# Sinkhorn attention and feed-forward on one core: the first half of w_in loaded in 16 equal pieces ahead of four pieces of queries

## The chip, the cores and the metric

The kernel runs on one core of a Trainium2 chip. The metric is the device time of one execution in microseconds (us). Five engines work side by side: TensorE (PE, with its weight loads shown as PEld), VectorE (DVE), ScalarE (ACT), GpSimd (POOL) and SyncE (SP). POOL and SP also issue DMA transfers, which 16 DMA engines carry out.

## What is computed

For each of 4 batches and 8 heads (768 tokens, head size 64) an 8x8 matrix is normalised five times over rows and columns. It mixes the 8 blocks (96 tokens each) of keys and values, and each block of queries attends to its mixed block. The result, 3072 tokens by 512, then goes through a feed-forward layer.

```
P = sort_net;  5 times: P = exp(P - max);  P /= rows' sums;  P /= columns' sums
k_s, v_s = P mixes the 8 blocks of k and of v
attn = softmax(q_b @ k_s.T / 8) @ v_s            per block of 96 tokens
h = x @ w_in;  g = s * relu(h)**2 + b;  out = g @ w_out
```

w_in is 512 x 2048 and w_out is 2048 x 512, both in fp32. The inputs' DMAs, issued by POOL, convert to bf16 on the way, so a piece that is 128 KB in memory lands as 64 KB. The profile counts what lands.

## The kernel before, in words

The order of every engine's work is written out by hand. A batch is cut into two halves of 384 tokens; a half is one "tile" t of the feed-forward layer, so there are eight tiles.

**Start.** PE runs dummy matmuls (`warm`, L131) while DVE and ACT normalise the 8x8 matrices (L257 to L272). In the meantime POOL issues loads in this order: the first half of the first queries (`load_qh(0, 0)`, L148 and L103), the first keys in 3 pieces (L149, L92), some small constants, and then the loads that the change touches (L163 to L171, all issued by `load_wi`, L141, and `load_qh`, L103). After them come memsets for the next batch (L172 to L175), the scalars s and b (L177), w_out in 4 pieces (L180), and values, keys and queries of batch 1 (L181 to L184).

**The queue.** Every transfer that POOL issues takes one of eight semaphores in turn. So a transfer can be issued only when the eighth one before it has landed; POOL waits there, and everything behind it on POOL's queue waits too.

**First half of batch 0.** L501 to L529: the mixing matrix (`build_pd`, L278), transposed queries (`q_banks`, L233), mixed keys (L303, L315) and values (L325), scores (L357, L375), the exponentials on ACT (L361, L380), weighted values (`p_piece`, L399), their transposes (`t_piece`, L416), and the first parts of the feed-forward product with w_in (`part`, L450), which use columns 0 to 511 of w_in. Dummy matmuls (L393, L445) are mixed in.

**Feed-forward, tile 0.** `ffn1(0)` (L593) walks over eight steps i, each with 256 columns of w_in. Step 0 is followed by `q_banks(0, 1)`, which reads the second half of the first queries. Steps 2 and 3 need columns 512 to 1023, steps 4 to 7 the second half of w_in. The second half of batch 0's attention is laid between the steps. `ffn1(1)` follows, with `make_bias` (L554) in step 4, which needs all of w_out; then `ffn2(0)` and `ffn2(1)` (L474) with batch 1's keys, values and queries between them, and so on for the other batches.

The array `wi` holds w_in as `[128, 4, 2048]`: index 1 is the quarter a of the 512 rows. `load_wi(f0, f1, a)` loads columns f0 to f1 of one or more quarters. W8 is 256 columns and W4 is 512.

Of the kernel before, what the change touches and what calls it, by code (L numbers as in the profile page):

```python
# [22 lines left out]
def kernel(  # L23
# [18 lines left out]
    NHP = H // 2  # L42
# [54 lines left out]
    def load_qh(b, half, parts=1):  # L97
        if b not in QH:
            QH[b] = rawp.tile([128, H, CQ, D], BF, tag="rawq", name="qh")
        qv = q[b].rearrange("h (f p c) d -> f p h (c d)", f=2, c=CQ)  # L100
        for h in range(0, H, H // parts):
            hs = slice(h, h + H // parts)
            nc.gpsimd.dma_start(  # L103
                out=QH[b][half * 64:(half + 1) * 64, hs].rearrange("p h c d -> p h (c d)"),
                in_=qv[half][:, hs])
# [33 lines left out]
    def load_wi(f0, f1, al=None):  # L139
        al = slice(0, NHP) if al is None else al  # L140
        nc.gpsimd.dma_start(out=wi[:, al, f0:f1], in_=wiv[:, al, f0:f1])  # L141
# [18 lines left out]
    ones = const.tile([128, 32], BF)  # L160
    W4 = d_ff // 4
    W8 = d_ff // 8
    for a in range(NHP):  # L163
        load_wi(0, W8, slice(a, a + 1))
    for a in range(0, NHP, 2):
        load_wi(W8, W4, slice(a, a + 2))
    for c in range(1, 4):
        for a in range(NHP):
            load_wi(c * W4, (c + 1) * W4, slice(a, a + 1))
        if c == 1:  # L170
            load_qh(0, 1, 2)  # L171
    nc.gpsimd.memset(ones, 1.0)  # L172
    nc.gpsimd.memset(VP[1][:, :, C2:GAP], 0.0)
    nc.gpsimd.memset(KS[1][:, :, :, C2:GAP], 0.0)
# [479 lines left out]
```

## Time and profile before

| | |
|---|---|
| runs | 232.03, 232.33 and 235.20 us; median 232.33 |
| the profiled execution, its own time | 235.48 us |
| its span, first to last instruction | 233.7 us |
| PE busy | 223.0 us (95% of the span) |
| DVE, ACT, POOL busy | 120.5, 100.4, 77.9 us |
| DMA issued by POOL ("software dynamic") | 12.85 MB landed in 25312 packets |
| DMA that brings instructions, queue 8 | 21 packets, 0.34 MB |
| `wi` loads, as issued | 4 of 64 KB landed, 14 of 128 KB landed |
| `qh` loads of batch 0 | one of 384 KB, two of 192 KB landed |

The profiled execution lies 1.78 us above its span and 3.15 us above the median; one of the three plain runs, 235.20 us, is close to it. In the views a row names the line, the engine, the operation, and what it writes and reads; "idle before" is how long the engine stood still ahead of it, followed by what ended the wait. "issue" stands for a wait whose end the profile can't put down to anything it shows. "PEclk" is the granted TensorE clock as a share of full speed. The DMA share can pass 1.00 because packets of one DMA engine overlap.

### The profile page before, as it was taken

To read this page: it belongs to the slowest core of one execution; us is meant where nothing else is said; L and a number is where in the kernel's file an instruction comes from. 1 tells how busy PE (TensorE), PEld (TensorE's weight loads), DVE (VectorE), ACT (ScalarE), POOL (GpSimd) and SP (SyncE) were. 2 spreads that over 40 slices of the span, in tenths; PEclk is the share of its full clock that TensorE was granted. 3 is DMA by queue.
4 is the path that set the end of the run, shared out by engine and by line. 5 is a ranking of instruction groups with operands and counts; after the bars stand their busy time and mean duration, and the time that the engine had idled before them with its cause. 6 is when DMAs were issued, how large, how long until landed. Compare 5 with 4: busy or idle time off the path is not lost.

```text
span 233.7 us, 6179 instructions
## 1 busy us (share of the span) xinstructions
PE 223.0 (95%) x2713; PEld 134.7 (58%) x2713; DVE 120.5 (52%) x237; ACT 100.4 (43%) x135; POOL 77.9 (33%) x131
## 2 busy tenths in 40 slices
PE   7977599799999999999999999999999999999994
PEld 5876356555565656566555555666465556654453
DVE  6686135559552665544454774546255754442221
ACT  4777178464125254565112436564015346660000
POOL 7666961603994792199100000003700000000000
PEclk9999889999999999999999999999999999999999
DMA  6999999990059996799911149000112430001112
GB/s 164 272 171 147 158 163 205 202 195 5 20 94 191 216 186 159 90 134 177 141 48 48 51 134 212 12 3 3 45 50 88 113 100 17 1 0 45 63 74 91
DMA packets 45243, 25.05 MB, mean 107 GB/s; under 512 B 29856, under 2 KB 41376, under 8 KB 45216
## 3 DMA queue, kind: packets, MB, share of 16 engines
q0 software_dynamic: 25312, 12.85, 42.4%
q1 hardware_dynamic: 19904, 11.81, 17.9%
q8 instruction: 21, 0.34, 0.6%
q14 instruction: 6, 0.05, 0.1%
HBM read 27.27 MB, written 6.29 MB: 144 GB/s over the span
## 4 chain that ended last, share of the span: by engine, by line
PE 93%; ACT 2%; issue 2%; DVE 1%
PE hps L450 37%; PE ops L474 35%; PE z L131 5%; PE tv L325 4%; PE pv L399 4%; PE sc L357 2%; PE tp L303 2%; PE ops L487 2%; ACT vs L206 1%; PE tqa L219 1%; PE pe L278 1%; PE scb L375 1%; PE tr L416 1%; ACT ks L206 0%; PE cps L554 0%
## 5 line engine op out<-in xcount | busy, mean ns | idle before, releaser
L450 PE MATMUL hps<-xt,wi 128*128 128x384 bf16 x512 | 88.1, 330 | 1.3 <-DVE xt L208 1.3
L474 PE MATMUL ops<-wo,gt 128*128 128x512 bf16 x368 | 85.5, 380 | 0.0
L462 ACT ACTIVATE rt<-hps 128x768 bf16<-128x768 f32 x64 | 51.9, 812 | 40.5 <-PE hps L450 39.9
L450 PEld LDWEIGHTS <-wi 128*128 128x128 bf16 x512 | 49.3, 99 | 33.8 <-issue 2.8
L463 DVE TENSOR_TENSOR gt<-rt 128x768 bf16<-128x768 bf16 x64 | 36.4, 570 | 46.9 <-ACT rt L462 46.6
L474 PEld LDWEIGHTS <-gt 128*128 128x128 bf16 x368 | 33.7, 98 | 36.7
L495 DVE SCALAR_TENSOR_TENSOR ot<-ops,s_bc,bias 128x512 f32<-128x512 f32 (+1 forms) x25 | 18.2, 728 | 36.3 <-PE ops L474 34.1
L405 DVE TENSOR_TENSOR x<-pv,rec 96x512 bf16<-96x512 f32 x32 | 22.0, 686 | 1.1
L365 ACT ACTIVATE at<-sc 112x768 bf16<-112x768 f32 x16 | 12.1, 808 | 21.0 <-PE sc L357 21.0
L200 POOL COPY vp<-rawv 128x384 bf16<-128x384 bf16 x24 | 19.1, 847 | 0.0
L399 PEld LDWEIGHTS <-at 112*128 112x128 bf16 (+1 forms) x256 | 13.0, 101 | 10.2 <-issue 3.5
L399 PE MATMUL pv<-vs,at 112*128 112x66 bf16 (+1 forms) x256 | 14.1, 195 | 3.4 <-issue 3.4
L538 POOL COPY scr<-gt 128x1 bf16<-128x1 bf16 x2 | 0.4, 189 | 49.2 <-DVE gt L463 49.2
L206 ACT CAST vs<-tv 112x1024 bf16<-112x1024 f32 (+1 forms) x7 | 6.3, 899 | 23.5 <-PE tv L325 23.5
L208 DVE CAST vs<-tv 112x1024 bf16<-112x1024 f32 (+1 forms) x11 | 12.0, 1123 | 6.2 <-PE tv L325 6.2
L92 POOL DMA_DIRECT2D rawk<-in_k_dram x21 | 11.3, 552 | 5.8 <-DMA wo<-in_moe_w_out_dram 4.9
L115 POOL DMA_DIRECT2D qtok<-in_q_dram x16 | 12.3, 781 | 2.2 <-issue 2.2
L141 POOL DMA_DIRECT2D wi<-in_moe_w_in_dram x18 | 10.1, 573 | 5.9 <-DMA rawk<-in_k_dram 2.7
L92 POOL DMA_DIRECT2D rawv<-in_v_dram x18 | 9.7, 580 | 6.7 <-DMA wo<-in_moe_w_out_dram 3.6
L131 PE MATMUL z<-zeros 128*64 128x96 bf16 (+2 forms) x130 | 10.7, 255 | 1.2 <-DVE zeros L119 1.2
L404 DVE RECIPROCAL rec<-pv 96x8 f32<-96x8 f32 x32 | 6.4, 200 | 10.0 <-PE pv L399 10.0
L208 DVE CAST ks<-tp 128x1024 bf16<-128x1024 f32 x8 | 9.4, 1220 | 2.0 <-PE tp L303 1.8
(83 smaller groups left out, 148.8 us busy)
## 6 DMA issues: line engine op xcount, KB each, us to landing
out_dram<-ot SPq DMA_DIRECT2D x23, 256.0 KB, 2.0
rawv<-in_v_dram POOLq DMA_DIRECT2D x18, 128.0 KB, 7.3
rawk<-in_k_dram POOLq DMA_DIRECT2D x18, 128.0 KB, 4.9
wo<-in_moe_w_out_dram POOLq DMA_DIRECT2D x4, 512.0 KB, 9.1
wi<-in_moe_w_in_dram POOLq DMA_DIRECT2D x14, 128.0 KB, 6.9
v0f<-in_v_dram SPq DMA_DIRECT2D x4, 384.0 KB, 5.9
qtok<-in_q_dram POOLq DMA_DIRECT2D x16, 96.0 KB, 4.9
qh<-in_q_dram POOLq DMA_DIRECT2D x3, 384.0 KB, 7.7
```

The lines of the kernel that those rows point to most:

```text
L92: nc.gpsimd.dma_start(out=ti[:, c:c + n, :].rearrange("p c d -> p (c d)"), in_=raw["qkv".index(t)][b][:, c * D:(c + n) * D])
L115: nc.gpsimd.dma_start(out=ti[:, n + h], in_=qv[:, n + h])
L131: nc.tensor.matmul(out=z[0:m, 0:w], lhsT=zeros[:, 0:m], rhs=zeros[:, 0:w], start=True, stop=True)
L200: eng.tensor_copy(out=o, in_=i)
L208: nc.vector.tensor_copy(out=out, in_=in_)
L399: nc.tensor.matmul(out=pv[0:m, e, n * VW:(n + 1) * VW], lhsT=atf[:, c0:c0 + m], rhs=VS[b % 2][:, e * NG + g0 + n, :], start=True, stop=True)
L405: nc.vector.tensor_tensor(out=x[:, :, hp * 128:(hp + 1) * 128].rearrange("p n (e d) -> p e n d", e=2), in0=pvv[:, :, :, 0:D], in1=rec.unsq ...
L450: nc.tensor.matmul(out=H1[t, i][:, f, 0:TG], lhsT=wi[:, hp, fc:fc + 128], rhs=XT[t][:, :, hp, :], start=(hp == 0), stop=(hp == NHP - 1))
L462: nc.scalar.activation(out=rt, in_=h, func=AF.Relu)
L463: nc.vector.tensor_tensor(out=gt[:, 2 * i:2 * i + 2, :], in0=rt, in1=rt, op=ALU.mult)
L474: nc.tensor.matmul(out=ops, lhsT=gt[:, f, m * 128:(m + 1) * 128], rhs=wo[:, f, :], start=(f == 0), stop=(f == NF - 1))
L495: nc.vector.scalar_tensor_tensor(out=ot[:, ns], in0=ops, scalar=s_bc, in1=BIAS[0][:, ns], op0=ALU.mult, op1=ALU.add)
```

## The change

The first 1024 columns of w_in come in 16 transfers of one row quarter and 256 columns each (128 KB in memory), column block by column block. Before, these columns came in 10 transfers: 4 of 128 KB, 2 that took two row quarters together (256 KB), and 4 of one row quarter and 512 columns (256 KB). Behind them the second half of the first queries comes in 4 transfers of two heads, no longer in 2 of four heads. The second 1024 columns keep their 8 transfers of 256 KB. In all POOL issues 24 `wi` transfers for 18, and 5 `qh` transfers of batch 0 for 3: eight more. The order of the bytes stays the same, and no other engine's instructions change.

```diff
-    for a in range(NHP):
-        load_wi(0, W8, slice(a, a + 1))
-    for a in range(0, NHP, 2):
-        load_wi(W8, W4, slice(a, a + 2))
-    for c in range(1, 4):
+    for c in range(4):
+        for a in range(NHP):
+            load_wi(c * W8, (c + 1) * W8, slice(a, a + 1))
+    load_qh(0, 1, 4)
+    for c in range(2, 4):
         for a in range(NHP):
             load_wi(c * W4, (c + 1) * W4, slice(a, a + 1))
-        if c == 1:
-            load_qh(0, 1, 2)
```

## Prediction

> **What bounds the kernel now.** I read the page first: PE is busy for 95% of the span and carries 93% of the chain that ended last, so a gain must come from a place where PE stands still or runs slowly. The change touches only loads of the first 24 us, so I then read the chain in order of time from 10 to 36 us:
>
> ```profile
> 9.97 1.91 PE z L131 x18
> 17.26 0.60 issue
> 22.39 0.13 PE pv L399 x4
> 22.52 3.38 issue
> 25.90 0.31 PE pv L399 x4
> 27.51 1.28 PE hps L450 x4
> 29.11 1.84 PE hps L450 x6
> 30.95 0.88 PE tqb L233 x48
> 33.83 1.41 PE hps L450 x8
> ```
>
> Up to 22.5 us no load of w_in is on the chain. Then PE stops for 3.38 us in the middle of one `p_piece`, between two matmuls of the same line whose inputs are long there; a shorter stop of the same kind stands at 17.26. The views of the DMA queues in two windows, 17 to 23.6 us and 23.6 to 24.7 us, say what comes late:
>
> ```profile
> q0 software_dynamic: 1151, 0.95, 109.6%
> q14 instruction: 1, 0.01, 0.9%
> ...
> q0 software_dynamic: 224, 0.20, 115.3%
> q8 instruction: 1, 0.02, 5.3%
> ```
>
> Queue 8 carries PE's code: its 21 packets over the whole span stand against 5426 PE instructions (2713 matmuls, 2713 weight loads), 258 each, and 0.34 MB / 21 is 16 KB. One such packet moved in 15 to 17 us, none from 17 to 23.6, one in the window that follows; PE starts again at 25.90, 1.2 us after that window. The two stops lie about 254 PE instructions apart (954 and 700 of them started), one packet's worth. So I read both stops as code that arrives late, behind software transfers that fill the DMA engines. After the stop the clock falls (stretches; the columns are us, busy time of PE, PEld, DVE, ACT, POOL, then the clock, DMA share, GB/s):
>
> ```profile
> 23.90:27.32 3.42, 1.42 (x21) 1.17 (x22) 0.89 (x2) 0.48 (x1) 3.27 (x8) 1.00 1.21 193
> 27.32:30.73 3.41, 3.41 (x18) 1.63 (x15) 0.00 (x0) 0.96 (x2) 3.41 (x6) 0.50 0.63 93
> 30.73:34.10 3.37, 3.37 (x69) 2.14 (x69) 1.58 (x3) 2.73 (x4) 1.78 (x5) 1.00 1.16 177
> ```
>
> Last, POOL in order of time:
>
> ```profile
> 9.72 0.71 POOL L141 DMA_DIRECT2D wi<-in_moe_w_in_dram  x1 [1.24 <-DMA qh<-in_q_dram]
> 11.11 0.71 POOL L141 DMA_DIRECT2D wi<-in_moe_w_in_dram  x1 [0.68 <-DMA rawk<-in_k_dram]
> 13.83 2.28 POOL L141 DMA_DIRECT2D wi<-in_moe_w_in_dram  x4 [2.02 <-DMA rawk<-in_k_dram]
> 16.08 1.30 POOL L103 DMA_DIRECT2D qh<-in_q_dram  x2
> 17.31 1.69 POOL L141 DMA_DIRECT2D wi<-in_moe_w_in_dram  x3
> 22.98 0.53 POOL L141 DMA_DIRECT2D wi<-in_moe_w_in_dram  x1 [0.45 <-DMA qh<-in_q_dram]
> 23.60 0.97 POOL L173 MEMSET vp<- 128x1024 bf16 x1
> 27.22 3.02 POOL L180 DMA_DIRECT2D wo<-in_moe_w_out_dram  x4
> ```
>
> From 13.83 POOL hands out 128 KB (landed) per 0.54 us, about 240 KB/us, more than the 199 KB/us that the DMA engines move in the full stretch from 24 to 25 us; that is how the queue gets deep. Its landing times grow to 7.9 us (median of the `wi` issued from 17 to 23.6 us), where one transfer of 128 KB on an empty queue takes 3.4 us (`rawk`, issued at 65.66).
>
> **The change, part by part.**
>
> *Issue on POOL.* Eight more transfers, 0.53 to 0.55 us each (`wi`, L141): 4.3 us of issue. The three issues at 9.72, 11.11 and 13.83 wait for the same first landings as now. From 14.5 on I count 0.535 us per `wi` and 0.57 per query piece (between 0.53 and the 0.68 of today's larger ones): the 16th piece of w_in goes out at 18.8, the queries at 19.3 to 21.6, the last `wi` at 25.3 to 25.9. That is 2.35 us behind today's 23.5, not 4.3, because today's waits (1.85 us in five pieces from 19.2 to 23) go: the transfer eight places ahead has by then landed. Memsets, s, b, w_out and batch 1's loads behind it on POOL's queue move by these 2.35 us.
>
> *The software queue.* A 64 KB piece every 0.535 us is 120 KB/us; in 14 to 15 us, where 64 KB pieces are moved, the rows show 192 KB/us. So POOL, not the DMA engines, now sets the pace from 14 to 19 us, and what is queued drains. At 13.83 six wi transfers are ahead, 384 KB now for 512; that is gone by about 17.5. Today the eight in flight at 18 us hold about 1 MB.
>
> *The code for PE.* It is asked for when PE reaches the block before, about 17 us by the count of instructions. Today it moves at 23.6, more than 6 us later; with an empty queue, code packets later in the trace follow within about 0.2 to 1.3 us of the same place in the count. I expect it by 19 to 20, in time for 22.5. The stop is worth between 0 (still late) and 3.38; I take 3.38 on the profiled execution, as the queue's rate is nearer to "drained" than to "full". The stop at 17.26 waits for an earlier packet with 128 KB less ahead of it (0.67 us at 192 KB/us): between 0 and 0.60, I take 0.3.
>
> *The half clock.* It follows 2 us of idle in one 3.4 us stretch. Ten matmuls of L450 take 3.12 us there (0.31 each) against 0.176 in the later row (8 in 1.41): 1.36 us; the ends are 0 and half the stretch, 1.7. I take 1.4. [...]
>
> *The later transfers.* The queries are next to be late. `q_banks(0, 1)` stands at 30.88 and would move up to about 25.8. The last piece is issued at 21.0; with 3.4 us (empty queue) it lands at 24.4, with 5.8 (today's two) at 26.8, with 8.2 (the longest `qh`) at 29.2. PE's wait is thus 0 to 3.4 us; I take 0, as the queue then holds little. Columns 512 to 1023 land by about 22 (needed 26.6), the second half of w_in by 30 (needed from 30.8, its last quarter from about 34.7). w_out's last piece lands near 42 today, so near 45, for L554 at 51.8 minus 5; batch 1's keys by 52.4 for L303 at 59.4 minus 5. All stay hidden, by about 2 us where it is tightest; without that cover the cost is the shift, up to 2.35.
>
> [...]
>
> **The sum.** 235.48 - 3.38 - 1.4 - 0.3 = 230.4 us for the profiled execution. The median lies 3.15 lower, so it cannot be known to have all of these losses. If it lacks none, it would go to 232.33 - 5.1 = 227.2; if the 3.15 are wholly these losses, 1.9 remain, 230.4. I take the half clock as absent from the median run (1.4 of the 3.15): it follows a stretch that was idle for 2.0 of its 3.42 us, so a stop that lies a little otherwise against the stretch, or a shorter one, may not bring it. Half of the other 1.75 I take as a shorter stop: 3.38 - 0.9 = 2.5, plus 0.3. That gives 232.33 - 2.8 = 229.5 us.
>
> **The rivals.**
>
> *The queries come late* (chance 0.14): they land around 27, PE waits some 1.5 us at L233 and half the gain returns, 231.0. For it: landings of 5.8 and 8.2 us in this trace. Against it: those had a full queue.
>
> *The code load doesn't depend on the queue* (0.15): the stop stays, the added issue is hidden: 232.3. For it: from 34 to 42 us the queue is just as full, and PE never stops there. Against it: PE runs long matmuls there and uses up its code more slowly.
>
> *Slower* (0.13): the code keeps its place behind the same bytes. Today it moves after the last query transfer (issued 16.7). The same bytes are now issued until 21.6, paced by POOL, and land about 1.3 us later than today's. Then the stop grows by 1.3 us: 233.6. It decides if code is served in order behind the queries and not when the engines run empty.
>
> **How the numbers follow.** The forecast, 229.5, has 0.58, with its own range of 227.2 to 230.4. The range for all, 228.0 to 232.8, reaches over the second and third case and leaves out the slower one and the lower end: 0.13 and 0.07. Faster by over 2% is under 227.7: 0.08, the case where the median has every loss. Slower by over 2% is above 237.0: 0.03. Within 2%, about what a measurement of this kernel can tell from no change: 0.89.
>
> **What would show it.** Right: no "issue" stop over 1 us on PE from 20 to 27 us, a code packet of queue 8 between 17.5 and 21, clock 1.00 to 34 us, `q_banks` (L233) near 26, the last L141 ending near 25.9, and w_out issued near 29.6. Wrong: the stop still there, or a new wait at L233 on `qh`, or POOL's loads more than 3 us later with PE waiting for `wi`, `wo` or `rawk`.

## The result and the profile after

The changed kernel takes 230.85 us (median of 18 runs, 230.03 to 232.06) against 233.08 us for the kernel before (18 runs, 232.03 to 237.31). The ratio is 0.9888, 95% interval 0.9864 to 0.9912: 1.1% faster. (Ratios here and below go by the fast runs alone, so they can differ a little from the quotient of two medians, 0.9904 here.) The profiled execution took 232.06 us with a span of 230.3.

The chain of the changed kernel in order of time, from 8 to 36 us (start, us, what; lines from L163 on have moved up by two):

```profile
2.62 9.65 DMA v0f<-in_v_dram
16.63 0.34 PE scb L373 x8
17.02 1.31 issue
18.34 0.30 PE sc L355 x6
18.64 1.75 PE tv L323 x64
24.11 0.27 PE pv L397 x8
24.38 0.17 PE tr L414 x4
27.53 0.88 PE tqb L231 x48
```

The stop of 3.38 us in the middle of the fourth `p_piece` is gone: its eight matmuls (24.11) now run without a break. The earlier stop is still there, and in this execution it is longer, 1.31 us for 0.60. The transposes of the queries (now L231) start at 27.53 instead of 30.95 on the chain, 3.4 us earlier, the difference between the two spans. Their inputs are not late: PE waits for no `qh`. Not all of this need be the change's doing: held up by the longer first stop and by the slow stretch shown next, PE came to the place of the old stop at 24.0 us for 22.3, where code that was a little late could no longer stop it. Two profiles of the same kernel with a short first stop are in the table below (e7, e10).

The stretches of the changed kernel (us; busy time of PE, PEld, DVE, ACT, POOL; clock, DMA share, GB/s):

```profile
15.33:18.75 3.42, 1.54 (x74) 1.25 (x68) 2.13 (x2) 2.19 (x6) 3.42 (x7) 1.00 0.92 113
18.75:22.16 3.41, 3.41 (x85) 2.98 (x80) 1.41 (x3) 2.47 (x5) 3.41 (x7) 0.50 1.04 130
22.16:25.57 3.41, 3.41 (x61) 2.88 (x59) 3.17 (x8) 1.93 (x5) 3.39 (x7) 1.00 1.02 119
```

A stretch at half clock is there too, but earlier, behind the first stop: PE was busy for 1.54 of the 3.42 us ahead of it. Most other runs of the changed kernel have none. Of its 30 runs in this study 6 show a mean clock of 0.993 or less, which is at least one such stretch (half of 3.41 us is 0.7% of the span); of 41 runs of the kernel before whose clock is known, 28 do.

POOL's timeline in the changed kernel:

```profile
11.07 0.53 POOL L141 DMA_DIRECT2D wi<-in_moe_w_in_dram  x1 [2.59 <-DMA qh<-in_q_dram]
14.79 4.76 POOL L141 DMA_DIRECT2D wi<-in_moe_w_in_dram  x9 [0.73 <-DMA rawk<-in_k_dram]
19.47 2.51 POOL L103 DMA_DIRECT2D qh<-in_q_dram  x4
21.84 4.44 POOL L141 DMA_DIRECT2D wi<-in_moe_w_in_dram  x8
30.00 3.02 POOL L178 DMA_DIRECT2D wo<-in_moe_w_out_dram  x4
```

From 14.79 on POOL never waits until 26.28: issuing is what takes its time, and the transfers behind are 2.8 us later (w_out at 30.00 for 27.22).

### The profile page after: what moved, and what is told of

Same layout as the page of the kernel before. It is cut to its first block, busy times and chain, and to the rows that moved or that the text cites. A ratio compares the mean times of both kernels' runs of the same rounds, so it can differ in the third digit from the quotient of the medians.

```text
span 230.3 us, 6164 instructions
## 1 busy us (share of the span) xinstructions
PE 219.7 (95%) x2690; PEld 134.4 (58%) x2713; DVE 120.6 (52%) x237; ACT 100.2 (43%) x135; POOL 81.8 (36%) x139
## 4 chain that ended last, share of the span: by engine, by line
PE 89%; DMA 4%; ACT 2%; issue 2%; SPq 1%; DVE 1%
PE hps L448 37%; PE ops L472 34%; DMA v0f<-in_v_dram 4%; PE tv L323 4%; PE pv L397 4%; PE sc L355 2%; PE tp L301 2%; PE ops L485 2%; PE scb L373 1%; PE tqa L217 1%; PE pv L391 1%; ACT vp L196 1%; SPq L80 1%; PE tr L414 1%; PE pe L276 0%
## 5 line engine op out<-in xcount | busy, mean ns | idle before, releaser
L448 PE MATMUL hps<-xt,wi 128*128 128x384 bf16 x512 | 86.6, 326 | 1.3 <-DVE xt L206 1.3
L472 PE MATMUL ops<-wo,gt 128*128 128x512 bf16 x346 | 81.5, 379 | 2.2 <-issue 1.6
L448 PEld LDWEIGHTS <-wi 128*128 128x128 bf16 x512 | 48.8, 98 | 33.2 <-issue 1.9
L141 POOL DMA_DIRECT2D wi<-in_moe_w_in_dram x24 | 12.9, 566 | 4.7 <-DMA qh<-in_q_dram 2.6
L323 PEld LDWEIGHTS <-vp 128*64 128x64 bf16 x512 | 9.4, 117 | 2.9 <-issue 2.1
L131 PE MATMUL z<-zeros 128*64 128x96 bf16 (+2 forms) x129 | 9.8, 242 | 1.3 <-DVE zeros L119 1.2
```

The source lines that it names most:

```text
L323: nc.tensor.matmul(out=ps[z * GAP:(z + 1) * GAP, d, :], lhsT=VP[b % 2][:, d0 + d, :], rhs=PD[b][:, :, z, :], start=True, stop=True)
L448: nc.tensor.matmul(out=H1[t, i][:, f, 0:TG], lhsT=wi[:, hp, fc:fc + 128], rhs=XT[t][:, :, hp, :], start=(hp == 0), stop=(hp == NHP - 1))
L472: nc.tensor.matmul(out=ops, lhsT=gt[:, f, m * 128:(m + 1) * 128], rhs=wo[:, f, :], start=(f == 0), stop=(f == NF - 1))
```

## The experiments

Theory: PE's code comes in packets of 16 KB (queue 8: 0.34 MB in 21 packets); a packet waits behind the software transfers already handed to the DMA engines; the change keeps fewer bytes ahead of it. For each run below, "second stop" is the break after PE's 478th weight load.

### The two parts alone

The w_in part alone (e1, and e8 later), as a diff against the change:

```diff
-    load_qh(0, 1, 4)
+    load_qh(0, 1, 2)
```

> Only the w_in part of the change: 16 pieces for the first half, the queries still in 2 transfers. Theory (PE's code packet waits behind the software transfers queued on its DMA engine; small pieces keep that queue short): the stop of over 3 us on PE near 22.5 us goes, ratio to the kernel before 0.985 to 0.992, like the whole change. Rival (the query pieces bring the gain): the stop stays, ratio 0.997 to 1.003.

Measured: 229.81 us, ratio 0.9815 (0.9737 to 0.9893); no second stop. That is more than expected, but all seven runs of the kernel before on this chip had a stretch at half clock, and none of e1's four. The query part alone (e2) keeps all w_in transfers:

```diff
         if c == 1:
-            load_qh(0, 1, 2)
+            load_qh(0, 1, 4)
```

> Only the query part of the change: w_in as before, the second half of the first queries in 4 transfers. Theory: two more issues of 0.55 us behind an already deep queue change little, the stop of 2 to 4 us near 22.5 us stays, ratio 0.995 to 1.005. Rival (the query pieces bring the gain): ratio 0.985 to 0.992.

Measured: 231.71 us, ratio 0.9895 (0.9831 to 0.9959). This was missed: the query part alone helps as well. Its chain still has the second stop, but shorter:

```profile
17.32 0.49 issue
22.47 1.18 issue
```

I read the reason as the limit of eight transfers in flight (in the kernel before the ninth issue, at 9.72 us, waited for the first landing). Four query pieces of 96 KB take four of the eight places; two of 192 KB took two, and two pieces of w_in of 128 KB stood in the others. So the query split, too, puts fewer bytes ahead of the code (0.43 MB in flight for 0.54, table below).

### The same transfers, handed out more slowly

e3 splits nothing. POOL does a memset (`hold`, on a tile that nobody reads) after each of six transfers, the four of columns 512 to 1023 and the two of queries, whose loop is written out for it:

```diff
+    def hold(n):
+        nc.gpsimd.memset(pace[:, 0:n], 0.0)
...
             load_wi(c * W4, (c + 1) * W4, slice(a, a + 1))
+            if c == 1:
+                hold(512)
...
                     in_=q[0].rearrange("h (f p c) d -> f p h (c d)", f=2, c=CQ)[1][:, hs])
+                hold(512)
```

> The transfers of the kernel before, none split, but POOL does a memset of about 0.5 us after each of the 4 pieces of columns 512 to 1023 and each of the 2 query transfers, so that it hands out about 125 KB/us as the changed kernel does. Theory (the depth of the queue counts, not the size of a transfer): the stop near 22.5 us goes or is under 1 us, ratio 0.985 to 0.993. Rival (small transfers in themselves let the code through, the queue's depth does not count): the stop stays at 2 to 4 us and the later issue gives 0.998 to 1.005.

Measured: 231.32 us, ratio 0.9875 (0.9794 to 0.9955). The second stop is gone with 128 KB pieces too, so small transfers are not needed to let the code through; handing out the same ones more slowly is enough. Nor does it take another order of the bytes: the change does alter it a little (columns 512 to 1023 come in two column blocks, before one row quarter at a time), e3 doesn't. The first stop was 1.32 us here, as in the profile of the change, and held PE up in the same way:

```profile
17.76 1.32 issue
```

### Moving the ends of the code packets

e4 leaves all loads alone and takes 176 PE instructions out of the dummy work at the start:

```diff
-    warm(108, 96, 64)
+    warm(20, 512, 64)
```

> All loads as before. The 108 dummy matmuls of 96 columns at the start become 20 of 512 columns (about the same 5 us of PE time): 176 PE instructions fewer ahead of the real work, so the ends of the code packets fall 176 instructions later in the work. Theory (the stops are ends of code packets): nothing stops in the fourth p_piece near 22.5 us any more; the stop lies 176 instructions later in the work, in or near the second p_piece near 21 us and near 33 us, and is shorter, under 1.5 us each, since by then the queue is older; ratio 0.985 to 0.995. Rival (PE waits there for data or for another engine): the stop stays at the same place in the work, at 3 us, ratio 0.998 to 1.002.

Measured: 236.81 us, ratio 1.0122 (1.0043 to 1.0202). PE in order of time:

```profile
15.65 0.23 PE L325 MATMUL tv<-pd,vp 128*64 128x64 bf16 x3
17.95 0.80 PE L325 MATMUL tv<-pd,vp 128*64 128x64 bf16 x29 [2.07 <-issue]
22.04 0.40 PE L399 MATMUL pv<-vs,at 112*128 112x66 bf16 x7
25.18 0.29 PE L399 MATMUL pv<-vs,at 112*96 112x66 bf16 x1 [2.74 <-issue]
```

The stops have left their places: one now lies inside the second `v_piece`, the other inside the first `p_piece`, ahead of the last of eight matmuls, whose inputs the seven others share. Counted from the program's start they lie after weight loads 223 and 350; in the kernel before they lay after 351 and 478. These are steps of 127 or 128 weight loads, 254 to 256 instructions, one 16 KB packet. So the place is set by the count of instructions and not by any data: the theory's main claim holds, the rival falls. One stop kept its count (350 for 351), which lies 176 instructions further on in the work, as expected. The rest was wrong: I had not counted on a stop at the packet's end before it (223), the expected one near 33 us did not come, I had both under 1.5 us, and I expected a faster kernel. With fewer dummy instructions PE gets to an end of a packet earlier in time relative to the loads, and the half clock came twice (18.29 and 25.11 us).

### Fewer and larger, and many more

e5 goes the other way:

```diff
-    for c in range(1, 4):
+    load_wi(W4, 2 * W4)
+    load_qh(0, 1)
+    for c in range(2, 4):
         for a in range(NHP):
             load_wi(c * W4, (c + 1) * W4, slice(a, a + 1))
-        if c == 1:
-            load_qh(0, 1, 2)
```

> The opposite of the change: columns 512 to 1023 in one transfer (4 before) and the second half of the first queries in one (2 before); the rest as before. The eight transfers that POOL may have in flight then hold more bytes when PE asks for its code near 17 us. Theory (the depth of the queue in bytes sets when the code comes): the stop after the 478th weight load gets longer than the 3.4 us of the first profile or stays near it, 3 to 6 us, ratio 1.000 to 1.020. [...]

Measured: 232.95 us, ratio 0.9971 (0.9927 to 1.0015). That lies below the range I expected, but isn't clear of no change. I expected a longer stop; in the profile it was 1.46 us, shorter than the 3.38 before:

```profile
22.00 1.46 issue
```

Each of these stops is from one execution: e5's was the fastest of its ten runs (231.66 us, no half clock), while that of the kernel before (235.48 us) was slower than 53 of its 59 other runs. So the difference may lie between executions and not between the kernels. In any case e5 doesn't support the theory that the bytes in flight set the wait: as PE passed the 351st weight load, 0.99 MB were in flight, against 0.54 in the kernel before (table below), and the next code packet came sooner, 4.70 us later instead of 6.61. While it waited, the queues moved more per us; first the kernel before (17.05 to 23.66 us), then e5 (16.45 to 21.15 us):

```profile
DMA packets 1152, 0.96 MB, mean 145 GB/s; under 512 B 97, under 2 KB 1151, under 8 KB 1151
DMA packets 1034, 0.90 MB, mean 191 GB/s; under 512 B 31, under 2 KB 1033, under 8 KB 1033
```

Faster movement may be why, but that isn't shown.

e6 takes the split further, as a diff against the change:

```diff
-    for c in range(4):
+    for c in range(8):
         for a in range(NHP):
-            load_wi(c * W8, (c + 1) * W8, slice(a, a + 1))
+            load_wi(c * W8 // 2, (c + 1) * W8 // 2, slice(a, a + 1))
```

> The change taken further: the first half of w_in in 32 transfers of 128 columns (16 in the change), the queries in 4. Sixteen more issues of 0.53 us: 8.5 us of POOL. Theory: the stops on PE's code stay away or short, but the queries are now issued near 28 to 30 us and land near 32 to 33, while PE wants them near 27: a wait of 4 to 6 us at L233, ratio to the kernel before 1.00 to 1.02. Rival (POOL's issue is hidden anyway): ratio 0.985 to 0.992 as with 16 pieces.

Measured: 239.67 us, ratio 1.0246 (1.0190 to 1.0302), a little slower than the expected 1.00 to 1.02. The chain, 24 to 40 us:

```profile
23.55 4.23 POOL wi L141 x8
27.78 1.58 POOL qh L103 x3
29.37 3.62 DMA qh<-in_q_dram
32.99 0.04 issue
33.03 0.53 PE tqb L231 x12
```

The code came soon (2.40 us after A, table below), but POOL's issue is now the chain: the queries go out at 27.58 to 30.2 us and PE waits 5.6 us for them (in four waits, the longest 4.5), and the clock then falls by half for two stretches (30.95 to 37.77). That is the rival "the queries come late", with its price; 16 pieces stay short of it, 32 do not.

### The change and its first part, five rounds on one chip

> The changed kernel itself once more, beside the w_in part alone. Theory: 0.984 to 0.992.

> The w_in part alone once more, five rounds, beside the whole change on the same chip. Theory (with 16 pieces the queue is short already, the query split adds two issues and nothing else): the same as the whole change within 0.4%. Rival (the query split costs or brings something of its own): apart by more than 0.4%.

Measured: the change 230.43 us, 0.9859 (0.9809 to 0.9910); the w_in part alone 230.40 us, 0.9856 (0.9805 to 0.9906). They are the same: with w_in in 16 pieces the query split adds nothing that can be measured.

### No split, with work that is needed anyway

e9 keeps the 20 transfers as they were and moves the four memset steps between the pieces of columns 512 to 1023:

```diff
+    between = [lambda: nc.gpsimd.memset(VP[1][:, :, C2:GAP], 0.0),
+               lambda: nc.gpsimd.memset(KS[1][:, :, :, C2:GAP], 0.0),
+               lambda: fill_vs(1),
+               lambda: nc.gpsimd.memset(ones, 1.0)]
     for c in range(1, 4):
         for a in range(NHP):
             load_wi(c * W4, (c + 1) * W4, slice(a, a + 1))
+            if c == 1:
+                between[a]()
...
-    nc.gpsimd.memset(ones, 1.0)
-    nc.gpsimd.memset(VP[1][:, :, C2:GAP], 0.0)
-    nc.gpsimd.memset(KS[1][:, :, :, C2:GAP], 0.0)
-    fill_vs(1)
```

> All 18 w_in and 2 query transfers of the kernel before, unsplit; the four memset steps that stood behind them (2.6 us of POOL, needed anyway) are moved between the 4 pieces of columns 512 to 1023. Theory (the bytes ahead of the code packet decide): fewer bytes are handed out by 18 us, the packet moves by about 20 us after 0.3 to 0.5 MB, the stop after the 478th weight load is under 0.5 us, ratio to the kernel before 0.983 to 0.991, like the change and without any added issue; w_out goes out near 27 us as before. Rival (splitting itself is needed): the stop stays at 1.5 to 3.5 us, ratio 0.996 to 1.003.

> The changed kernel beside the moved memsets on the same chip. Theory: the same as the moved memsets within 0.4%, 0.984 to 0.990 to the kernel before.

Measured on the same chip: e9 231.06 us, 0.9909 (0.9875 to 0.9943); the change 230.36 us, 0.9882 (0.9830 to 0.9933). The second stop is gone in e9 as well, without any added issue (w_out goes out at 28.02 us, for 27.22 before and 30.00 with the change). What stays is the first (e9's chain):

```profile
16.73 1.18 issue
17.91 0.30 PE sc L359 x6
```

Half of e9's 12 runs show a clock of 0.993 or less, as can come behind a first stop of this size; of the change's 6 runs beside it two do. e9 and e3 keep the two 128 KB transfers ahead of this stop, which the change splits; whether that is the reason isn't shown, as the change's own first stop was 1.31 us in one profile and 0.4 to 0.7 in two others. No version tried is clearly faster than the change.

### All runs in one table

PE passes the 351st weight load at A (in e4 the 223rd, and its second stop is the one after the 350th); the next code packet starts at B. In flight at A is what POOL had finished issuing by then, less what the software queue had moved. The bytes moved from A to B are those of the queues' view; the rest is from the instruction and packet records of each profile.

| kernel | A | B | B - A | MB in flight at A | MB moved, A to B | second stop |
|---|---|---|---|---|---|---|
| e4, 88 dummy pairs fewer | 15.65 | 22.80 | 7.15 | 0.49 | 1.20 | 2.74 |
| before | 17.05 | 23.66 | 6.61 | 0.54 | 0.95 | 3.38 |
| e5, coalesced | 16.45 | 21.15 | 4.70 | 0.99 | 0.89 | 1.46 |
| e9, memsets between | 16.53 | 20.75 | 4.22 | 0.16 | 0.43 | none |
| e2, queries only | 17.12 | 21.21 | 4.09 | 0.43 | 0.63 | 1.18 |
| after | 16.82 | 20.59 | 3.77 | 0.12 | 0.44 | none |
| e3, paced | 17.56 | 21.00 | 3.44 | 0.29 | 0.44 | none |
| e7, the change again | 16.46 | 19.54 | 3.08 | 0.16 | 0.35 | none |
| e1, w_in only | 16.62 | 19.04 | 2.42 | 0.11 | 0.28 | none |
| e6, 32 pieces | 17.16 | 19.56 | 2.40 | 0.05 | 0.15 | none |
| e8, w_in only | 17.19 | 19.56 | 2.37 | 0.16 | 0.27 | none |
| e10, the change again | 16.74 | 18.78 | 2.04 | 0.16 | 0.22 | none |

With 0.43 to 0.99 MB in flight the packet came 4.1 to 7.2 us after A, with 0.05 to 0.29 MB 2.0 to 4.2 us. So the packet comes late where much is in flight; within each group, though, the wait doesn't follow the bytes. The bytes moved from A to B are no cause: they include transfers issued after A, and a longer wait moves more of them by itself.

PE starts again 1.2 to 1.5 us after a packet has ended wherever it stood waiting for it (24.60 to 25.90 in the kernel before, 22.14 to 23.65 in e2, 23.80 to 25.18 in e4). Where there is no second stop, the packet had ended 1.2 to 2.5 us before PE came to the place, so the shortest margins are just enough. In the change's first profile, e3 and e9 PE came there at 23.5 to 24.0 us, held up by the long first stop; in e1, e7, e8 and e10 it came at 21.8 to 22.5, as in the kernel before (22.3), and the code was there in time without that help.

## Why the prediction was right, point by point

**Direction and size.** 229.5 us and a ratio of 0.988 to the median shown then; measured 230.85 and 0.9888. The sum for the profiled execution, 230.4, lies near the later profiles without a half clock (229.80 and 229.88 us, e7 and e10), not near the first one (232.06). Part of the distance of 1.35 us is the reference: over 18 runs the kernel before has a median of 233.08, 0.75 above the one I started from.

**The stop is late code, behind the software queue.** Shown: e4 moves it by the count of instructions, e3 and e9 shorten the packet's wait (4.22 and 3.44 us for 6.61) without splitting anything, and e6 shows what remains with little ahead. How the wait follows from the bytes is not shown (e5). The packet started at 20.59 in the profile of the change, inside the 17.5 to 21 that I gave, though later than my "19 to 20"; in e7 and e10 it started at 19.54 and 18.78. With the packet's own 0.95 us and the 1.2 to 1.5 us until PE restarts, a start by 20 is just in time for 22.5, and one at 20.59 is not; in that profile PE came only at 24.0.

**POOL sets the pace.** Right: 0.51 to 0.54 us from one `wi` piece to the next but for one, 0.12 MB in flight at A for 0.54, last `wi` ended at 26.28 (25.9 predicted), w_out at 30.00 (29.6).

**The queries are not late.** Right at 16 pieces; e6 shows the cover's end. Their transposes start at 25.27 and 25.32 in e7 and e10 (near 26 predicted), at 27.53 in the first profile, behind its long first stop and its half clock.

**The first stop, 0.3 us to be gained.** Not confirmed. It was 1.31 us in the profiled change, but 0.4 to 0.7 in e1, e7, e8 and e10, against 0.60 before. It varies from run to run. I put that down to the loads of the start, which land differently even before anything has changed, but no run tests it: the first `qh` had landed by 9.72 in one profile and by 11.07 in the other, judged by the issue that waits for it; the chain of the changed kernel begins with the values' load `v0f`, which landed only at 12.27.

**The half clock, 1.4 us, taken as absent from the median run of before.** This step failed. 28 of 41 runs of the kernel before show it (7 of 7, 13 of 17 and 8 of 17 on three chips), so the usual run has it. Its size was right: the change's 6 runs with one such stretch have a median 1.4 us above its 24 without. In runs with a clock of 0.998 or more, medians are 232.5 us (13 runs of before) and 230.6 (24 of the change): 1.9 us with no half clock on either side, which I read as what the stop costs in such runs, so it is there usually shorter than 3.38. The rest of the gain, a few tenths in the medians, is that the stretch at half clock comes in 6 of 30 runs instead of 28 of 41. So my 2.8 us stand against 2.2 in the medians: 2.5 for the stop against some 1.9, 0.3 for the first stop against nothing shown, and 0 for the clock against a few tenths. That the total came so close is in part luck: too much for the stops, nothing for the clock.

**Clock 1.00 to 34 us in the profile.** Wrong for the profiled execution (0.50 from 18.75 to 22.16); it fell behind the first stop, which I had expected to shrink.

## What to carry to other kernels

Here a stop on PE marked "issue" in the middle of a run of equal matmuls (3.38 us), with another such stop 254 PE instructions away, was code that came late. To see whether a stop in another kernel is one too, take instructions out ahead of it, as e4 does, and look whether the place moves with the count. Here the code was late where over 0.4 MB of other transfers were in flight one packet earlier. What removed the stop was handing out the loads more slowly (e3, ratio 0.9875), splitting them with at most eight in flight (the change, 0.9888), or putting needed work between them (e9, 0.9909), as long as the issuing engine didn't then become the chain (24 `wi` and 4 query pieces were hidden, with 16 more the kernel was 2.5% slower than before). Take a second look at a stop of over a microsecond: behind those of 1.31 us (the change) and 1.18 us (e9) came a stretch at half clock, and the change's runs with such a stretch have a median 1.4 us above those without.

## What the runs showed of the hardware

PE's code moved in packets of 16 KB, 21 of them for the 5426 PE instructions of the kernel before: 258 each, beside 254 to 256 instructions between stops. A packet that came late stopped PE for 3.38 us in that kernel's profile and for 2.74 in e4's.

From PE's 351st weight load to the start of the code packet, 0.95 MB of the software queue moved in the kernel before, and 0.44 in the change's profile. Eleven of the twelve profiles look like one line: the packet started when the software queue had moved about what POOL had finished issuing as PE began the 352nd weight load (2.84 MB for 2.62 in the kernel before, 2.53 for 2.42 in e2; in e4, at the 224th, 2.93 for 2.88; never more than 0.22 apart). But the order isn't simply first come, first served: in e5 the packet started 0.36 MB sooner than that, and at 35.6 us in the kernel before, eight transfers of together 2.2 MB were in flight, and the next code packet, asked for about then by the count of instructions, moved at 38.70 after 0.64 MB. In which order the DMA engines serve the queues stays open; no run tried it.

A stop as short as 1.2 to 1.3 us, beside a wait of 0.6 us for ACT's evictions just ahead of it, was enough for a stretch of 3.41 us at half clock (the change's profile, and e9's), but not always: e3's of 1.32 us brought none. They divide by how long PE was busy within one stretch of the clock, 3.41 us: in the twelve profiles, between 8 and 40 us, every stretch at full clock with 1.68 us or less of PE work was followed by half clock, and none with 1.88 us or more. The rows are e9's (followed by half clock), then e6's and e3's (not followed):

```profile
14.93:18.35 3.42, 1.68 (x83) 1.38 (x77) 2.35 (x3) 2.32 (x6) 3.23 (x9) 1.00 1.14 155
24.12:27.53 3.41, 1.88 (x15) 0.94 (x12) 0.56 (x1) 1.77 (x3) 3.41 (x7) 1.00 0.69 62
17.48:20.90 3.42, 2.10 (x90) 1.78 (x89) 1.56 (x3) 2.02 (x4) 3.42 (x7) 1.00 1.00 129
```

So the longest of these three stops, e3's, had no half clock behind it, and the shortest, e9's of 1.18 us, had. The prediction had allowed for that: a stop that lies otherwise against the stretch may not bring it.
